# Other PSUM banks for two h groups of the first chunk, turns of pair 1 moved together, and one weight cast from VectorE to ScalarE

## The chip, the cores and the metric

The kernel runs on one core of a Trainium2 chip. The metric is device time in microseconds (us) of one execution; lower is better. Several executions are taken of each kernel, and fast ones are compared with fast ones. Times inside an execution count from the first instruction of its trace. The program names the engines PE (TensorE's matmuls), PEld (its weight loads), DVE (VectorE), ACT (ScalarE), POOL (GpSimd) and SP (the queue that issues most DMA).

## The reference

```python
def _attn_ref(q, k, v):                       # 8 batches, 8 heads, 576 positions, 64 dims
    q_p, k_p = phi(q, cos_w, sin_w), phi(k, cos_w, sin_w)   # phi: concat(relu(x)*cos, relu(x)*sin)
    kv  = einsum('bhsf,bhsd->bhfd', k_p, v)
    num = einsum('bhsf,bhfd->bhsd', q_p, kv)
    den = einsum('bhsf,bhf->bhs', q_p, k_p.sum(2))[..., None] + 1e-06
    return num / den

def _moe_ref(x, w_in, w_out, beta):           # x: 4608 x 512, w_in: 512 x 2048, w_out: 2048 x 512
    h = x @ w_in
    return (h * (1.0 / (1.0 + exp(-beta * h)))) @ w_out
```

The output of the attention is the x of the second function.

## The kernel before

The second function runs in nine chunks of 512 tokens: 16 h groups (each 128 columns of h, in one PSUM bank), each through ScalarE, then the products with w_out (`o_mm`). TensorE is kept busy with these while the attention of later batches is slipped in between. The first batch has nothing to hide behind: its attention is the head of the kernel, cut into two halves by heads ("pair 0", "pair 1"), so that the first h groups can begin on pair 0's half of the contraction. The parts concerned:

```python
    def h_bank(c, jt):                       # which PSUM bank an h group fills
        if c < 2 and jt < 4:
            return ((3, 2, 0, 1), (6, 7, 4, 5))[c][jt]
        ...
    # head of the kernel, batch 0; turns are TensorE transposes, copied out by ScalarE
    x_turn_pe(0, 0, 4, 4, jps=(0,))          # pair 0, blocks 0-3, into bank 4
    x_turn_pe(0, 4, 8, 5, jps=(0,))          # pair 0, blocks 4-7, into bank 5
    for n in range(7):
        num_mm(n, 1, 0, n)                   # num of pair 1 ("num 1"): banks 0 and 1
    num_mm(7, 1, 6, 0)                       # its eighth block: banks 6 and 7
    for gj, eng in zip(GJ, ("pool", "dve", "pool", "dve")):
        cast_win(0, gj, eng, jps=slice(0, 1))
    for gj, eng in zip(GJ, ("dve", "pool", "pool", "pool")):
        cast_win(0, gj, eng, jps=slice(1, 2))
    got = x_rden(0, 0, 0, 7, (1,))           # den and its reciprocal, VectorE, from banks 0 and 1
    x_mul(got, 0, 4)                         # num / den, VectorE
    x_mul(got, 4, 7)
    x_mul(x_rden(6, 0, 7, 8, (1,)), 7, 8)
    for jt in range(3):
        h_mm(0, jt, (0, 1))                  # h groups on pair 0: banks 3, 2, 0
    x_turn_pe(0, 0, 4, 4, ("act",), (1,))    # turns of pair 1
    h_mm(0, 3, (0, 1))
    x_turn_pe(0, 4, 8, 5, ("act",), (1,))
    ...
    def rest():                              # after h group 4
        ...
        load_w("out", 0); load_w("out", 1)
        load_raw(1, "v"); load_raw(1, "k"); load_raw(1, "q")
        x_turn_dma(0, 8, 9)                  # DMA transpose
        load_w("out", 2, 2); load_w("out", 3, 2)
        ...
        v_scale(1, 0); k_relu(1); q_relu(1, 0); q_relu(1, 1)
    def second():                            # after the products of slot 23
        takes.append(q_turn_pe(1, 1, 6, hold=True))
        cast_out(8)                          # first cast of w_out 2, VectorE
        takes[0]("act", 0)                   # pair 0 of q out of PSUM: copies on ScalarE,
        takes[0]("dve", 1)                   # multiplies by tan on VectorE
        cast_out(9, "a")
        takes[0]("dve", 0)
        ...
    early = {                                # what follows which slot of chunk 0
        22: lambda: (kv_mm(1, 0, 6), kv_mm(1, 1, 6), kv_take((0, 1), 6, "act"),
                     takes.append(q_turn_pe(1, 0, 4, hold=True))),
        23: second,
        24: lambda: (num_seven(0, 4), x_mul(x_rden(4, 0, 0, 7, (0,)), 0, 7)),
        ...
    }
```

## Time and profile before

| | before |
|---|---|
| time, median (lowest to highest) of the 4 executions given with the result | 295.78 us (295.52 to 296.08) |
| span of the profiled execution, granted clock | 294.0 us, 0.997 |
| TensorE busy; its share of the chain that ended last | 96%; 91% |
| VectorE, ScalarE, GpSimd busy | 39%, 48%, 26% |
| third h group waits, at 19.21 us | 1.35 us |
| the relu of batch 1's q on VectorE starts; TensorE turns it | 39.43 us; 40.66 us |

The busy shares say which engine bounds most of the span.

### The profile page before, as it was taken

What the parts mean: (1) busy time and instruction counts of PE and PEld (TensorE: products, weight loads), DVE (VectorE), ACT (ScalarE), POOL (GpSimd) and SP (SyncE); (2) the same over time, 40 slices, a digit from 0 to 9 for tenths busy, and PEclk for the clock granted to TensorE, in tenths of its full rate; (3) what the DMA queues carried; (4) which work ended last, traced back from release to release, by engine and by line L of the source; (5) the groups of instructions that cost most, each with busy time, mean ns of one, the idle gap of its engine ahead of it and who ended that gap; (6) DMA issues with size and microseconds to landing.
All of it is one profiled execution on the core that took longest, in us unless ns stands there. A gap on an engine that the chain in (4) does not pass through costs nothing.

```text
span 294.0 us, 7191 instructions
## 1 busy us (share of the span) xinstructions
PE 282.8 (96%) x3047; PEld 143.5 (49%) x3074; DVE 115.2 (39%) x293; ACT 141.8 (48%) x225; POOL 75.5 (26%) x85
## 2 busy tenths in 40 slices
PE   8679999999999999999999999999999999999994
PEld 7454455455445544454445444454455444444444
DVE  5999976743910292029401950086005000000000
ACT  5748856862157324821483138412760177127511
POOL 1440000624381026402640255027701210000000
PEclk9999999999999999999999999999999999999998
DMA  7999999999998099906991699068102910131033
GB/s 256 365 393 384 392 305 389 278 230 352 165 268 347 3 140 231 393 30 131 222 391 47 125 229 401 34 74 198 36 2 41 154 36 0 38 79 28 0 74 71
DMA packets 50736, 53.89 MB, mean 183 GB/s; under 512 B 31232, under 2 KB 31632, under 8 KB 50704
## 3 DMA queue, kind: packets, MB, share of 16 engines
q1 hardware_dynamic: 47744, 45.95, 53.9%
q0 software_dynamic: 2688, 7.34, 10.5%
q8 instruction: 24, 0.39, 0.5%
q10 hardware_dynamic: 272, 0.14, 0.2%
q14 instruction: 8, 0.07, 0.1%
HBM read 36.71 MB, written 9.44 MB: 157 GB/s over the span
## 4 chain that ended last, share of the span: by engine, by line
PE 91%; DMA 3%; DVE 2%; issue 1%; SPq 1%; ACT 0%
PE ps L365 42%; PE ps L390 41%; PE ps L280 3%; DMA raw_v<-in_v_dram 3%; PE ps L259 3%; PE ps L408 1%; SPq L78 1%; DVE win L108 1%; DVE xs L302 1%; PE ps L339 0%; PE ps L229 0%; DVE rden L295 0%; DVE vb L204 0%; ACT xt L344 0%; DVE rk L189 0%
## 5 line engine op out<-in xcount | busy, mean ns | idle before, releaser
L365 PE MATMUL ps<-xt,win 128*128 128x512 bf16 (+1 forms) x580 | 127.8, 378 | 1.5 <-DVE xs L302 1.3
L390 PE MATMUL ps<-wout,g_t 128*128 128x512 bf16 x535 | 120.5, 379 | 2.5 <-issue 1.5
L372 ACT ACTIVATE g_t<-ps,beta 128x512 bf16<-128x512 f32 x144 | 98.6, 688 | 33.1 <-PE ps L365 33.1
L365 PEld LDWEIGHTS <-win 128*128 128x128 bf16 x580 | 56.1, 98 | 67.6 <-issue 2.1
L390 PEld LDWEIGHTS <-g_t 128*128 128x128 bf16 x560 | 53.9, 98 | 64.2 <-issue 0.9
L385 POOL DMA_DIRECT2D out_dram<-o_sb x56 | 39.2, 705 | 141.2 <-ACT o_sb L396 141.2
L396 ACT COPY o_sb<-ps 128x512 f32<-128x512 f32 x35 | 20.2, 588 | 98.7 <-PE ps L390 94.5
L271 DVE CAST kv<-ps 128x520 bf16<-128x520 f32 x6 | 4.2, 700 | 68.9 <-PE ps L259 68.9
L217 POOL TENSOR_TENSOR qs<-qt,tanr 128x1152 bf16<-128x1152 bf16 x12 | 28.4, 2384 | 9.3 <-DMA qt<-qb 7.8
L411 DVE COPY o_sb<-ps 128x256 f32<-128x256 f32 (+1 forms) x2 | 0.7, 358 | 62.7 <-PE ps L408 62.7
L302 DVE TENSOR_TENSOR xs<-ps,rden 128x768 bf16<-128x768 f32 (+5 forms) x27 | 23.1, 863 | 0.8
L291 DVE TENSOR_TENSOR den<-ps,eps 128x12 f32<-128x12 f32 (+4 forms) x26 | 4.2, 160 | 33.5 <-PE ps L280 33.5
L214 DVE TENSOR_SCALAR vb<-raw_v,cos 128x256 bf16<-128x256 f32 x63 | 17.1, 346 | 0.0
L214 DVE TENSOR_SCALAR vb<-raw_v,sin 128x256 bf16<-128x256 f32 x54 | 14.7, 347 | 0.0
L280 PEld LDWEIGHTS <-qt 64*64 64x64 bf16 x576 | 10.4, 106 | 4.7 <-issue 3.8
L108 DVE CAST win<-w_stage 64x512 bf16<-64x512 f32 x27 | 12.0, 443 | 0.6
L189 DVE TENSOR_SCALAR qb<-raw_q 128x1152 bf16<-128x1152 f32 x16 | 11.4, 752 | 1.8 <-DMA raw_q<-in_q_dram 1.8
L280 PE MATMUL ps<-kv,qt 64*64 64x65 bf16 x576 | 11.7, 195 | 0.5 <-ACT kv L269 0.5
L259 PE MATMUL ps<-vb,rk 64*64 64x130 bf16 x576 | 10.2, 218 | 1.9 <-ACT rk L187 1.3
L280 PE MATMUL ps<-kv,qs 64*64 64x65 bf16 x576 | 11.5, 193 | 0.0
L259 PEld LDWEIGHTS <-rk 64*64 64x64 bf16 x576 | 8.5, 106 | 5.8 <-issue 3.0
L280 PEld LDWEIGHTS <-qs 64*64 64x64 bf16 x576 | 10.4, 105 | 0.0
(58 smaller groups left out, 98.1 us busy)
## 6 DMA issues: line engine op xcount, KB each, us to landing
raw_v<-in_v_dram SPq DMA_DIRECT2D x7, 1152.0 KB, 10.3
raw_k<-in_k_dram SPq DMA_DIRECT2D x7, 1152.0 KB, 12.8
raw_q<-in_q_dram SPq DMA_DIRECT2D x7, 1152.0 KB, 7.1
out_dram<-o_sb POOLq DMA_DIRECT2D x56, 128.0 KB, 4.0
w_stage<-in_moe_w_in_dram SPq DMA_DIRECT2D x3, 1024.0 KB, 13.7
w_stage<-in_moe_w_out_dram SPq DMA_DIRECT2D x2, 1024.0 KB, 8.1
w_stage<-in_moe_w_out_dram SPq DMA_DIRECT2D x4, 512.0 KB, 11.2
out_dram<-o_sb SPq DMA_DIRECT2D x14, 128.0 KB, 2.3
```

Of the source, the lines that this page charges most:

```text
L108: nc.vector.tensor_copy(o, a)
L189: nc.vector.tensor_scalar(dst, src, scalar1=0.0, scalar2=None, op0=ALU.max)
L214: nc.vector.tensor_scalar(o, a, scalar1=t[:, n : n + 1], scalar2=None, op0=ALU.mult)
L217: eng.tensor_tensor(dst.rearrange("q n (g p) -> q n g p", g=2), src.rearrange("q n (g p) -> q n g p", g=2), tanr[:, n0:n1].unsqueeze(2).to ...
L259: nc.tensor.matmul(t[jj * HP : (jj + 1) * HP, g], lhsT=rk[hs, n, 2 * jp + jj, :], rhs=vb[hs, n, 2 * jp + jj].rearrange("q s e -> q (s e)") ...
L280: nc.tensor.matmul(ps[cols, bank + jj, slot * E : (slot + 1) * E], lhsT=(qt, qs)[cs][rows, jp, n, cols], rhs=kv[rows, g, jp, cs, :], start ...
L302: nc.vector.tensor_tensor(o.rearrange("q j n s d -> q j (n s) d"), nv[:, :, a:z, :, 0:D].rearrange("q j n s d -> q j (n s) d"), rden[:, :, ...
L365: nc.tensor.matmul(ps[:, h_bank(c, jt), blocks.start * 64 : blocks.stop * 64], lhsT=win[jt // 4][:, mi, (jt % 4) * P : (jt % 4 + 1) * P], ...
L372: nc.scalar.activation(g_t, ps[:, h_bank(c, jt)], AF.Silu, scale=beta[:, jt : jt + 1])
L385: eng.dma_start(out=out_v[bb, n][:, m0:m1], in_=o_sb[hf * HP : (hf + 1) * HP, m0:m1])
L390: nc.tensor.matmul(o_ps, lhsT=gs[c, jt][:, tt * P : (tt + 1) * P], rhs=wout[jt // 4][:, jt % 4, :], start=(jt == 0), stop=(jt == JT - 1))
L396: nc.scalar.copy(o_sb, o_ps)
```

## The change

The intent is to let the third h group run without waiting for num 1 to be read, to let both turns of pair 1 go ahead of the fourth group, and to start VectorE's work on num 1 one cast earlier.

```diff
     def h_bank(c, jt):
         if c < 2 and jt < 4:
-            return ((3, 2, 0, 1), (6, 7, 4, 5))[c][jt]
+            return ((3, 2, 5, 0), (6, 7, 4, 5))[c][jt]
...
-    warm_pe(8, 128, bank=2)
+    warm_pe(7, 128, bank=2)
...
-    for gj, eng in zip(GJ, ("dve", "pool", "pool", "pool")):
+    for gj, eng in zip(GJ, ("act", "pool", "pool", "pool")):
         cast_win(0, gj, eng, jps=slice(1, 2))
...
     x_turn_pe(0, 0, 4, 4, ("act",), (1,))
+    x_turn_pe(0, 4, 8, 1, ("act",), (1,))
     h_mm(0, 3, (0, 1))
-    x_turn_pe(0, 4, 8, 5, ("act",), (1,))
```

## The prediction

> **What bounds the kernel now.** I read the page first: engine shares and the chain that ended last.
>
> ```profile
> PE 282.8 (96%) x3047; PEld 143.5 (49%) x3074; DVE 115.2 (39%) x293; ACT 141.8 (48%) x225; POOL 75.5 (26%) x85
> ...
> PE 91%; DMA 3%; DVE 2%; issue 1%; SPq 1%; ACT 0%
> ```
>
> TensorE is busy in 96% of the span and carries 91% of the chain. The list of waits after 21 us shows nothing for TensorE but 1.5 us of "issue" in 8 places. So the change can win only in the head, before TensorE runs without a gap, and what it wins there reaches the end only if nothing later makes TensorE wait. The diff touches the stretch from 15 to 22 us. The timeline there, TensorE first (start, duration, instruction, idle before it and what ended that):
>
> ```profile
> 16.84 1.02 PE L365 MATMUL ps<-xt,win 128*128 128x512 bf16 x4
> 19.21 0.59 PE L365 MATMUL ps<-xt,win 128*128 128x512 bf16 x2 [1.35 <-DVE xs L302]
> 19.64 0.39 PE L339 MATMUL ps<-ident,xs 128*128 128x128 bf16 x4
> 19.87 0.59 PE L365 MATMUL ps<-xt,win 128*128 128x512 bf16 x2
> 20.30 0.39 PE L339 MATMUL ps<-ident,xs 128*128 128x128 bf16 x4
> 20.70 1.03 PE L365 MATMUL ps<-xt,win 128*128 128x256 bf16 x6
> ```
>
> The x4 at 16.84 are h groups 1 and 2 on pair 0. The third group (19.21) waits 1.35 us, though its data are ready: it goes to bank 0, which num 1 filled and VectorE's multiplies (L302) still read. VectorE and ScalarE in the same stretch:
>
> ```profile
> 16.14 1.48 DVE L108 CAST win<-w_stage 64x512 bf16<-64x512 f32 x2
> 17.55 0.15 DVE L291 TENSOR_TENSOR den<-ps,eps 128x14 f32<-128x14 f32 x1
> 17.73 0.24 DVE L295 RECIPROCAL rden<-den 128x14 f32<-128x14 f32 x1
> 18.00 1.16 DVE L302 TENSOR_TENSOR xs<-ps,rden 128x512 bf16<-128x512 f32 x2
> 19.08 0.15 DVE L291 TENSOR_TENSOR den<-ps,eps 128x2 f32<-128x2 f32 x1
> 19.26 0.17 DVE L295 RECIPROCAL rden<-den 128x2 f32<-128x2 f32 x1
> 19.46 0.29 DVE L302 TENSOR_TENSOR xs<-ps,rden 128x128 bf16<-128x128 f32 x1
> ...
> 20.07 1.24 ACT L344 COPY xt<-ps 128x512 bf16<-128x512 bf16 x2 [3.27 <-PE ps L339]
> ```
>
> num 1 is finished at 16.75 (its last matmuls start at 16.54 and take 0.21), but VectorE begins its den at 17.55: the second of the two casts, 16.90 to 17.62, stands in front. ScalarE is idle for 3.27 us. Both turns of pair 1 queue behind the blocked third group, and the chain runs from the second turn through ScalarE's second xt copy (20.72 to 21.31) to TensorE at 21.36, from where it is TensorE alone.
>
> The next view is a later one, around the second batch's q, because there data arrive by DMA:
>
> ```profile
> 39.51 1.22 PE L259 MATMUL ps<-vb,rk 64*64 64x130 bf16 x72
> 40.66 0.68 PE L229 MATMUL ps<-ident,qb 128*128 128x128 bf16 x9
> ...
> 39.43 1.43 DVE L189 TENSOR_SCALAR qb<-raw_q 128x1152 bf16<-128x1152 f32 x2 [1.48 <-DMA raw_q<-in_q_dram]
> 41.27 0.49 DVE L116 TENSOR_SCALAR wout<-w_stage,rbeta 128x512 bf16<-128x512 f32 x1 [0.41 <-DMA w_stage<-in_moe_w_out_dram]
> 41.67 1.42 DVE L217 TENSOR_TENSOR qs<-ps,tanr 128x512 bf16<-128x512 bf16 x2
> ```
>
> VectorE sits idle for 1.48 us until q of batch 1 lands at about 39.4; the first of its two relus ends at 40.19, and TensorE turns that result at 40.66. TensorE arrives only 0.47 us after the data. The table of stretches shows why that landing is what it is: DMA share 1.04 to 1.05 and 387 to 389 GB/s from 16.8 to 33.4 us.
>
> **What the Trainium skill says.** "PSUM — Partial Sum Buffer", § PSUM bank collisions raise a hardware error, asks for semaphores by bank and quadrant and not by address. That is the wait seen here: the third group writes columns that have nothing to do with the unread num, but the same bank; it starts at 19.21, 0.05 us after the multiply that reads bank 0 ends at 19.16. "SBUF — State Buffer", § Who interferes with whom: casts in VectorE's two-port mode and GpSimd share a port pair and exclude each other. The trace agrees: VectorE's cast takes 0.72 us in the stretch with GpSimd casting and 0.42 us (median) elsewhere. "ScalarE: Activation LUTs", § What ACT_TABLE_LOAD costs, gives 186 ns + 0.833 ns per element for immediate scale; the trace's ScalarE relu of 128x576 takes 0.667 us, the formula 0.666. So a 64x512 cast there is an estimate of 0.61 us. "DMA: Bandwidth & Descriptors", § Queues, rings and completion order: each DMA engine takes one queue's descriptors in ring order. The loads land in their order of issue here.
>
> **The change part by part.**
>
> 1. The cast moves. VectorE loses 0.72 us before den. The one remaining cast ends at 16.87, den can start as close behind it as now, at 16.79 (0.07 before the cast's recorded end), just after num 1. Everything through the last x_mul moves up by 17.55 - 16.79 = 0.75 us: first multiply done at 17.94, second at 18.41, eighth block at 19.00. ScalarE takes the cast at about 16.79 (after its two pair 0 copies, 15.72 + 1.07), done about 17.4, inside its idle 3.27 us: free. Its half of the weight has landed by then (VectorE's cast of it started at 16.90 without a wait, GpSimd's at 16.65).
>
> 2. Third group to bank 5. That bank held pair 0's second turn, copied out by 16.79. So the group follows at once: four matmuls at 0.215 us each from 16.84, then two more, to 18.13. The 1.35 us of idle is gone from there.
>
> 3. Turn order. First turn at 18.13 (xs ready 17.94), its four matmuls are issued in 0.22 us and drain to 18.52; ScalarE copies 18.55 to 19.14. The second turn in bank 1 must wait for the eighth block at 19.00: three of its four transposes earlier, the last at 19.05, drained at 19.27. ScalarE's second copy runs from 19.30 to 19.89. The fourth group (bank 0, free at 18.41) fills TensorE meanwhile: 2 x 0.215 from 19.11 to 19.54. Then four half-width matmuls of pair 1 at 0.108 each, to 19.97. The second copy is done by 19.94 with its signal, so no wait. TensorE thus enters its unbroken part at 19.97 in place of 21.36: **1.39 us gained locally.**
>
> 4. One fewer 128-wide warm-up matmul, 0.107 us at about 5 us. The chain there is DMA (V to 12.26), so it is worth 0.
>
> What becomes of 1.39 us later. VectorE's casts of w_in 1 to 3 can't move by 0.75: the first one's weights land at about 19.1 us, so they move by about 0.53. TensorE moves by 1.39 and the margins shrink by 0.86. The tightest are h groups 13 and 15 of chunk 0. Last cast for group 15: now 31.03, then 30.50; its second matmul, which needs it, now 31.86, then 30.47. With 0.05 for the signal that is a wait of some 0.08: gain 1.31.
>
> Then q of batch 1. Its landing doesn't move, since the queue ahead of it was never empty: the loads in front are issued 0.5 us earlier into a backlog of megabytes. kv_mm would start at 38.20 (its k_relu ends at about 37.85, good) and end at 39.35, but the relu of q still ends at 40.19, so the turn begins at 40.24, not 39.35. **Gain left: 40.66 - 40.24 = 0.42.** TensorE waits about 0.9 us there. A little after, num of pair 0 needs the tan multiplies on VectorE, which follow the cast of w_out 2 (its landing at 41.25 ends a DMA wait as well) and end at 43.09. Num starts at 43.49 now, so at earliest 43.14: **gain left 0.35.** The next dependences (second multiply of x ends at 48.92, turn at 49.47) leave 0.55, so they pass. From there on TensorE only moves: 295.89 - 0.35 = **295.54**, which I round to 295.5.
>
> **The rivals.**
>
> *All of it survives (294.6).* For: the chain now is TensorE alone from 21.36, which read naively promises the full 1.3. Against: a 0.47 us slack behind a DMA-limited landing. It would need q to land 0.9 us earlier. From 37 to 39 us DMA throughput falls under 200 GB/s around a DMA transpose, which VectorE triggers some 0.5 us earlier in the new kernel, so the landing could move, but the transpose's issue (25.85 to 31.6) already ends 5 us before.
>
> *Nothing gained, or slightly worse (295.9 to 296.1).* For: q, w_out 2 and the tan multiplies could be later by a few tenths in this run; ScalarE's cast could collide with the turns' copies, or the waits could be put on coarser signals than I assume. Against: ScalarE has 1.1 us between the estimate of its cast's end and the first turn copy.
>
> *The local gain is smaller (0.6 to 0.7).* If VectorE's den does not start at 16.79 because num 1's signal comes later, all shifts with it. But as anything from 0.42 upward is cut to 0.35 afterwards, the time would still be 295.5. The point estimate is robust in this direction.
>
> **Range and chances.** The before runs spread over 0.4 us (295.68 to 296.08). The capped gain of 0.35 is of that size; allow run scatter of about 0.4 above and, for the case that the landing moves, some 0.8 below: 294.7 to 296.1. Two per cent is 5.9 us, over four times the whole local gain, and nothing in the change adds work of that size: same 0.98, 0.01 for either side.
>
> **What would show it.** Right: third group at about 17.7 with no wait; den at 16.8; unbroken TensorE from about 20.0; then a new wait of 0.8 to 0.9 us before the turn of q at 40.2, ended by VectorE's relu behind a q landing still near 39.4; and num at 43.1. Wrong: if that wait is missing and q lands near 38.5, the time goes to 294.6; if TensorE waits in the w_in casts by more than 0.1, my 0.53 for VectorE was off; if the second copy on ScalarE ends after 20.0, the local gain is smaller, with little effect on the end.

## The result

| | before | changed |
|---|---|---|
| median (lowest to highest), 4 executions each | 295.78 us (295.52 to 296.08) | 295.09 us (294.92 to 295.44) |
| ratio, 95% interval | | 0.9978 (0.9960 to 0.9995) |
| span of the profiled execution | 294.0 us | 293.1 us |

A ratio is the mean time of one kernel's fast runs over the mean of the other's of the same rounds, so it is not quite the ratio of the medians. This one is 0.65 us (0.0022 x 295.8) in favour of the change, with an interval from 0.15 to 1.2 us.

The page of the changed kernel, busy times and the chain that ended last:

```profile
PE 282.5 (96%) x3046; PEld 143.2 (49%) x3073; DVE 115.0 (39%) x292; ACT 142.5 (49%) x226; POOL 73.3 (25%) x85
...
PE 84%; DMA 8%; DVE 3%; issue 1%; SPq 1%
PE ps L390 39%; PE ps L365 38%; DMA raw_q<-in_q_dram 5%; PE ps L280 3%; DMA raw_v<-in_v_dram 3%; PE ps L259 2%; DVE win L108 2%; PE ps L408 1%; SPq L78 1%; DVE xs L302 1%; PE ps L229 0%; DVE vb L204 0%; DVE rden L295 0%; PE ps L339 0%; DVE qb L189 0%
```

TensorE's busy time is the same to 0.3 us, but its share of the chain fell from 91% to 84%, and a load has come in with 5%: q. The chain no longer follows TensorE through the h groups of chunk 0; it goes through the landing of batch 1's q. The timeline of the head, TensorE, VectorE and ScalarE (start, duration, instruction, idle before it and its releaser):

```profile
16.54 1.46 PE L365 MATMUL ps<-xt,win 128*128 128x512 bf16 x6
17.83 0.80 PE L339 MATMUL ps<-ident,xs 128*128 128x128 bf16 x7
18.88 0.23 PE L339 MATMUL ps<-ident,xs 128*128 128x128 bf16 x1 [0.25 <-ACT xt L344]
18.95 1.90 PE L365 MATMUL ps<-xt,win 128*128 128x512 bf16 x12
...
16.60 0.17 DVE L291 TENSOR_TENSOR den<-ps,eps 128x14 f32<-128x14 f32 x1
17.08 1.16 DVE L302 TENSOR_TENSOR xs<-ps,rden 128x512 bf16<-128x512 f32 x2
18.53 0.29 DVE L302 TENSOR_TENSOR xs<-ps,rden 128x128 bf16<-128x128 f32 x1
...
16.38 0.62 ACT L104 CAST win<-w_stage 64x512 bf16<-64x512 f32 x1
19.15 0.58 ACT L344 COPY xt<-ps 128x512 bf16<-128x512 bf16 x1 [0.30 <-PE ps L339]
```

Six matmuls now follow each other at 16.54, the third group with them; seven of the eight turns come straight behind; ScalarE's cast takes 0.62 us in what was idle time. The "ACT" on the last turn is the wait's last semaphore as inferred, but that copy ends at 18.84; VectorE's last multiply, from which this turn reads, ends at 18.82 too, and I read the wait as its. The end of this stretch, where the half-width matmuls pass into the unbroken run, is 1.54 us earlier than before; but this execution also began earlier. The last turns before the change's first effect (15.28 us before, 14.98 here) are 0.30 us earlier already, because V landed earlier (VectorE's second product with it starts at 11.98 and not at 12.28). So the local gain is 1.54 - 0.30 = 1.24 us.

The stretch of batch 1's q, TensorE first and VectorE second:

```profile
37.98 1.22 PE L259 MATMUL ps<-vb,rk 64*64 64x130 bf16 x72
40.33 0.68 PE L229 MATMUL ps<-ident,qb 128*128 128x128 bf16 x9 [1.13 <-DVE qb L189]
43.22 0.22 PE L280 MATMUL ps<-kv,qt 64*64 64x65 bf16 x4
...
39.52 1.43 DVE L189 TENSOR_SCALAR qb<-raw_q 128x1152 bf16<-128x1152 f32 x2 [1.58 <-DMA raw_q<-in_q_dram]
41.35 0.48 DVE L116 TENSOR_SCALAR wout<-w_stage,rbeta 128x512 bf16<-128x512 f32 x1 [0.40 <-DMA w_stage<-in_moe_w_out_dram]
41.75 1.42 DVE L217 TENSOR_TENSOR qs<-ps,tanr 128x512 bf16<-128x512 bf16 x2
```

TensorE reaches the kv product 1.53 us earlier (39.51 to 37.98) and then stands 1.13 us in front of the turn, a wait that the kernel before doesn't have. At num it is 43.49 - 43.22 = 0.27 us ahead. The lead stays like that for 150 us. The other 0.6 us by which the two spans differ come from one place: the profile of the kernel before has a pause of TensorE at 193.6 us that this one lacks.

```profile
193.56 1.68 PE L390 MATMUL ps<-wout,g_t 128*128 128x512 bf16 x7 [0.40 <-issue]
```

Nothing in the profile releases it ("issue"). The experiments ask whether it belongs to the kernel or to the execution.

### The profile page after: what moved, and what is told of

Its sections match the earlier page's. It is cut to its first block, busy times and chain, and to the rows that moved or that the text cites. A ratio compares the mean times of both kernels' runs of the same rounds, so it can differ in the third digit from the quotient of the medians.

```text
span 293.1 us, 7188 instructions
## 1 busy us (share of the span) xinstructions
PE 282.5 (96%) x3046; PEld 143.2 (49%) x3073; DVE 115.0 (39%) x292; ACT 142.5 (49%) x226; POOL 73.3 (25%) x85
## 4 chain that ended last, share of the span: by engine, by line
PE 84%; DMA 8%; DVE 3%; issue 1%; SPq 1%
PE ps L390 39%; PE ps L365 38%; DMA raw_q<-in_q_dram 5%; PE ps L280 3%; DMA raw_v<-in_v_dram 3%; PE ps L259 2%; DVE win L108 2%; PE ps L408 1%; SPq L78 1%; DVE xs L302 1%; PE ps L229 0%; DVE vb L204 0%; DVE rden L295 0%; PE ps L339 0%; DVE qb L189 0%
## 5 line engine op out<-in xcount | busy, mean ns | idle before, releaser
L385 POOL DMA_DIRECT2D out_dram<-o_sb x56 | 37.2, 668 | 144.9 <-ACT o_sb L396 144.9
L108 DVE CAST win<-w_stage 64x512 bf16<-64x512 f32 x26 | 11.2, 433 | 0.6
L189 DVE TENSOR_SCALAR rk<-raw_k 128x2304 bf16<-128x2304 f32 (+2 forms) x9 | 10.5, 1172 | 0.6 <-DMA raw_k<-in_k_dram 0.6
```

The costliest lines, as they stand in the source:

```text
L108: nc.vector.tensor_copy(o, a)
L189: nc.vector.tensor_scalar(dst, src, scalar1=0.0, scalar2=None, op0=ALU.max)
L385: eng.dma_start(out=out_v[bb, n][:, m0:m1], in_=o_sb[hf * HP : (hf + 1) * HP, m0:m1])
```

## The experiments

**Theory.** The change wins about 1.25 us in the head, and two data limits between 40 and 43 us take most of it back: the relu of q behind q's landing, and, just behind, num behind the tan multiplies, which stand on VectorE behind the first cast of w_out 2 and so behind *its* landing. **Rivals:** every local gain counts in full; q is the only limit; q is late because of a DMA transpose; the profile's pause is a part of the kernel before.

All kernels gave correct results. Kernels share the runs of the kernel before: first four below (before 295.48 us), next four (295.45 us) and last four (295.29 us). "Ratio" is to those.

### The changed kernel again

No edit.

> The changed kernel once more, for a tighter interval. My theory (the local gain is cut where TensorE waits for q of batch 1): 0.27 to 0.40 us faster than before, ratio about 0.9989, and a wait of about 1.1 us before the turn of q. Rival (the full local gain of 1.3 to 1.5 us reaches the end in most executions and my one profile shows an unlucky q): about 1.3 us faster, ratio 0.9955. Rival (the first timing of 0.65 us is the true size, so there is a second gain after the wait): ratio 0.9978.

Measured: 294.69 us, ratio 0.9988 (0.9972 to 1.0003), so 0.35 us faster. The wait at the turn was 0.78 us, not the 1.1 that I expected; the relu of q started at 39.11, the turn at 39.93, num at 42.81. Each of the three is about 0.4 us earlier than in the first profile of the same kernel, while TensorE arrived at the kv product at the same time (37.94 and 37.98). So num follows the data one to one and not TensorE, which is what a limit does. (The cast of w_out 2 started 0.41 us earlier too, so this doesn't say which of the two landings sets num.) The full-gain rival is out for this kernel (1.3 us lies outside the interval); the timing alone doesn't separate 0.35 from 0.65.

### The cast alone

```diff
-    for gj, eng in zip(GJ, ("dve", "pool", "pool", "pool")):      # kernel before
+    for gj, eng in zip(GJ, ("act", "pool", "pool", "pool")):
```

> The kernel before with the cast on ScalarE alone; banks and turn order as before. Local gain by my theory: VectorE's den 0.75 us earlier, third group 18.45 in place of 19.21, unbroken TensorE about 0.75 us earlier. As 0.75 is more than the slack of 0.3 to 0.45 before the turn of q, the end gains as much as the whole change, 0.3 to 0.4 us, with a wait of about 0.4 us at the turn of q. Rival (every local gain counts in full): 0.75 us faster, half of what the whole change gives.

Measured: 295.00 us, ratio 0.9990 (0.9977 to 1.0002). TensorE in its head and at q:

```profile
18.46 0.59 PE L365 MATMUL ps<-xt,win 128*128 128x512 bf16 x2 [0.72 <-DVE xs L302]
...
38.76 1.22 PE L259 MATMUL ps<-vb,rk 64*64 64x130 bf16 x72
40.24 0.68 PE L229 MATMUL ps<-ident,qb 128*128 128x128 bf16 x9 [0.27 <-DVE qb L189]
```

The third group still waits for its bank, but half as long (0.72 us for 1.35). The execution began 0.13 us early, so the local gain is 39.51 - 38.76 - 0.13 = 0.62 us. A wait of 0.27 us at q is already there (0.4 expected), and num comes at 43.12 against 43.22 for the whole change. Half of the local gain gives all of the end gain.

### The banks and the order alone

```diff
-    for gj, eng in zip(GJ, ("act", "pool", "pool", "pool")):      # changed kernel
+    for gj, eng in zip(GJ, ("dve", "pool", "pool", "pool")):
```

> The change without its cast: that one stays on VectorE; banks and turn order are new. Local gain by my theory: the multiplies of pair 1 stay where they were, the third group runs before them at about 17.7, ScalarE's second copy ends at about 20.6 in place of 21.3, unbroken TensorE 0.65 us earlier. At the end 0.3 to 0.4 us, as the whole change, with a wait of about 0.3 us at the turn of q. Rival (every local gain counts in full): 0.65 us faster.

Measured: 294.55 us, ratio 0.9978 (0.9966 to 0.9990).

```profile
16.70 1.46 PE L365 MATMUL ps<-xt,win 128*128 128x512 bf16 x6
18.62 0.81 PE L339 MATMUL ps<-ident,xs 128*128 128x128 bf16 x7 [0.46 <-DVE xs L302]
...
38.76 1.22 PE L259 MATMUL ps<-vb,rk 64*64 64x130 bf16 x72
39.91 0.68 PE L229 MATMUL ps<-ident,qb 128*128 128x128 bf16 x9
```

The third group is free, and the wait has moved to the turn, which now waits for VectorE. Local gain 39.51 - 38.76 - 0.14 = 0.61 us. With the cast's 0.62 that makes 1.23, the whole change's 1.24: the two parts add up in the head. At the end they don't. The wait at q that I expected is missing: q's relu began at 39.09 in this execution, and the turn at 39.91 is 0.82 behind it, the same distance as where TensorE did wait (40.33 - 39.52 = 0.81). TensorE and data arrived together. As timed, this half of the change is no worse than the whole.

### The DMA transpose behind the loads of w_out

```diff
         load_raw(1, "q")                                          # changed kernel
-        x_turn_dma(0, 8, 9)
         load_w("out", 2, 2)
         load_w("out", 3, 2)
+        x_turn_dma(0, 8, 9)
```

> The changed kernel with the DMA transpose of the ninth block of batch 0 issued behind the loads of w_out 2 and 3 in place of in front of them, so that nothing slow follows q in the queue. If the landing of q of batch 1 limits, and the transpose delays that landing: q lands 0.5 to 1.0 us earlier (38.5 to 39.0), the wait at its turn shrinks from 1.1 to 0.2 to 0.6 us, and the time falls by 0.3 to 0.9 us below the changed kernel. Rival (q lands by bandwidth alone): landing near 39.4, same time as the changed kernel within 0.2 us.

Measured: 295.00 us, but six executions between 294.30 and 296.92; ratio 1.0003 (0.9976 to 1.0030). The relu of q started at 39.51: no earlier than before. The idea that the transpose delays q finds no support here, and the rival fits. One profile doesn't close it: its head was 0.66 us late (V's second product at 12.64 and not 11.98), and the least gain looked for, 0.5 us, lies within the scatter of q's landing (below). What did come earlier is w_out 2, now issued in front of the transpose (the queue begins with its loads at 27.40 and not 31.81): its cast follows the relus without a wait.

```profile
40.87 0.49 DVE L116 TENSOR_SCALAR wout<-w_stage,rbeta 128x512 bf16<-128x512 f32 x1
```

In the changed kernel it started at 41.35 behind the same relu (39.52) and the same turn of q (40.33 in both). Num starts at 43.16 here and at 43.22 there. So with q landing as late as this, the second limit costs only some 0.06 us more than the first.

Two of the executions were near 296.8, the profiled one among them, and it shows a new thing, TensorE in the middle of num of pair 1:

```profile
45.62 0.19 PE L280 MATMUL ps<-kv,qs 64*64 64x65 bf16 x1
47.37 0.22 PE L280 MATMUL ps<-kv,qs 64*64 64x65 bf16 x3 [1.55 <-issue]
```

TensorE stands still for 1.55 us between two matmuls of one product, with no data wait. The moved transpose runs just before: from 42.2 to 44.6 us the DMA engines are busy and move only 168 GB/s. Two packets of the DMA queues of kind "instruction" follow it, one between 44.5 and 45.0 us and one between 45.5 and 46.0; in the changed kernel the same two come some 2 us earlier (42.5 to 43.0 and 43.0 to 43.5). That TensorE's own instructions were late behind the transpose fits, but is argued and not shown: the view doesn't say for which engine a packet is.

### Four idle matmuls in the changed kernel, and in the kernel before

```diff
     early = {
+        10: lambda: warm_pe(4),          # 4 x 128x512 into bank 1, which nothing reads then
```

> The changed kernel with four idle 512-wide matmuls (4 x 0.216 = 0.86 us of TensorE) behind h group 11 of chunk 0. If TensorE has 0.8 to 1.1 us to spare before the turn of q: the wait there shrinks to 0 to 0.25 us, and the time is that of the changed kernel within 0.1 us. Rival (no slack; TensorE time counts in full): 0.86 us longer than the changed kernel.

> The kernel before with the same four matmuls. It has no wait for q, so both theories say the whole 0.86 us is paid (ratio to before 1.0029), at most 0.3 us less where q lands late in an execution; with the changed kernel's four matmuls free, the two kernels with matmuls differ by about 1.2 us, as much as the local gain of the change.

Measured: changed with matmuls 295.80 us, ratio 1.0007 (0.9992 to 1.0022), from five fast runs; its profiled execution fell into a throttled state (425 us at a granted clock of 0.66) and says nothing. Before with matmuls 296.88 us, ratio 1.0054 (1.0037 to 1.0071).

Both expectations were partly missed. The kernel before pays 1.6 us (0.0054 x 295.4) and not 0.86; the changed kernel pays about 0.6 to 0.9 us more than without them (ratios 0.9978 to 0.9988), and not nothing. The difference between the two kernels came out as expected, though: 1.0054 - 1.0007 = 0.0047, or 1.4 us, two to four times what separates them without the matmuls (0.0022 and 0.0012). That the change is then worth its whole local gain is nevertheless not shown by this, because part of the 1.4 us arises far behind q. The trace of the kernel before with matmuls shows where its excess went. TensorE reaches the kv product at 40.14; with 0.23 us for an early start that is 40.14 - 39.51 + 0.23 = 0.86, all of it as expected and without a wait for q. The rest came later, most of it in one pause of 0.49 us of idle, close to where the kernel before had paused:

```profile
193.88 0.22 PE L280 MATMUL ps<-kv,qs 64*64 64x65 bf16 x2 [0.49 <-issue]
```

From before this pause to behind it, the distance to the second profile of the kernel before (below) grows from 0.71 to 1.39 us. So 0.68 us of the excess is the pause, as far as this execution speaks for the others. Another thing differs in it: q's relu started only at 40.07, over 0.5 us later than in any other profile with q in one load. Whether the matmuls delayed the load or it is scatter isn't known.

### q of batch 1 in two halves

```diff
-        load_raw(1, "q")                                          # changed kernel
+        load_raw(1, "q", 0, 2)
+        load_raw(1, "q", 2, 4)
```

> The changed kernel with q of batch 1 loaded in two halves, so the relu and the turn of the first pair no longer wait for the whole of q: first half lands near 38.0 us, its relu ends at about 38.8, TensorE turns it at about 39.1 without a wait or with one under 0.2 us. By my second limit (the tan multiplies on VectorE stand behind the cast of w_out 2, which lands at 41.25) TensorE then waits about 0.6 us more at the group of w_out 2 or at num, which still starts at about 43.1: time equal to the changed kernel within 0.15 us. Rival (the wait for q is the only limit): 0.8 to 1.1 us faster than the changed kernel.

Measured: 294.99 us, ratio 0.9985 (0.9967 to 1.0003). The time is that of the changed kernel, as the second limit says. The profile couldn't show why, since this execution's head was late: V landed 1.06 us later than in the repeat below (second product at 13.11 and not 12.05), the granted clock was 0.64 between 16.0 and 19.2 us, and TensorE was at the kv product only at 40.09. So it was run once more (below).

### Halves, and both limits behind them moved

```diff
         takes.append(q_turn_pe(1, 1, 6, hold=True))               # kernel with halves
-        cast_out(8)
         takes[0]("act", 0)
         takes[0]("dve", 1)
-        cast_out(9, "a")
         takes[0]("dve", 0)
         takes[0]("act", 1)
+        cast_out(8)
+        cast_out(9, "a")
         cast_out(10)
...
         cast_out(11, "a")
-        cast_out(12)
-        for j in range(13, JT):
+        cast_out(12, "a")
+        num_seven(0, 4)
+        x_mul(x_rden(4, 0, 0, 7, (0,)), 0, 7)
+        cast_out(13)
+        for j in range(14, JT):
             cast_out(j, "a")
...
-        24: lambda: (num_seven(0, 4), x_mul(x_rden(4, 0, 0, 7, (0,)), 0, 7)),
```

> The same halves, with both limits behind q moved as well: the tan multiplies of pair 0 ahead of the cast of w_out 2 on VectorE, num of pair 0 ahead of the group of w_out 2 on TensorE, and pair 0's multiply of x ahead of a cast that waits for w_out 3 (casts 12 and 13 swapped between the engines). By the theory of queued limits: num of pair 0 at about 41.6 us, 0.6 to 1.0 us faster than the changed kernel, about 1.0 to 1.4 us faster than the kernel before (ratio 0.9955 to 0.9966). Rival (some further data limit within 0.2 us, such as w_out 3): equal to the changed kernel.

Measured: 294.54 us, ratio 0.9970 (0.9954 to 0.9985), so 0.89 us faster than the kernel before, a little short of the expected 1.0. Against the changed kernel (0.9988 and 0.9978), that is 0.2 to 0.5 us and not the 0.6 to 1.0 that I expected. It is 0.0015 better than the halves alone, which the intervals don't secure. The trace does show the effect:

```profile
39.25 0.68 PE L229 MATMUL ps<-ident,qb 128*128 128x128 bf16 x9
41.52 0.22 PE L280 MATMUL ps<-kv,qt 64*64 64x65 bf16 x4 [0.23 <-DVE qs L217]
```

No wait at the turn of q, num at 41.52 as expected (it stands ahead of one 0.86 us group there, so its time isn't compared with the others' directly). The first h group of chunk 1 starts at 50.47 us; before it started at 51.59 and with the change at 51.31. So it keeps 1.12 us where the change keeps 0.28 (these two executions began 0.18 and 0.30 us early). It has the lowest ratio, though its interval overlaps with that of the banks and order alone (0.9966 to 0.9990).

### The kernel before again

No edit.

> The kernel before, for a second profile of it. Its first profile has a pause of TensorE of 0.56 us at 193.6 us that no other kernel's profile has at that place. If the pause belongs to the execution and not to the kernel, it is missing here and the span is about 293.4 us in place of 294.0; if it belongs to the kernel, it is here again, and the change removed it.

Measured: 295.29 us, span 293.5 us. The pause at 193.6 us is not there. It belonged to the execution. The two profiles of the kernel before agree within 0.05 us up to num (turn of q at 40.61, num at 43.45). So of the 0.9 us between the first two spans, about 0.5 us (294.0 - 293.5) was this pause and not the change.

### Halves again, and the changed kernel with matmuls again

The edits are those above.

> The kernel with q in two halves once more, because its first profile fell in an execution in which TensorE ran at half rate between 17 and 19 us and so arrived too late for any wait to show. Expected where the head runs at full rate: no wait or one under 0.2 us at the turn of q, then a wait of 0.5 to 0.7 us at the group of w_out 2 or at num; num at about 43.1 us, time equal to the changed kernel. Rival: num at about 42.2 us.

Measured: 294.83 us, ratio 0.9986 (0.9968 to 1.0005), a head at full clock, and the expected picture:

```profile
39.19 0.68 PE L229 MATMUL ps<-ident,qb 128*128 128x128 bf16 x9
...
42.77 0.22 PE L280 MATMUL ps<-kv,qt 64*64 64x65 bf16 x4 [0.31 <-DVE qs L217]
...
40.90 0.49 DVE L116 TENSOR_SCALAR wout<-w_stage,rbeta 128x512 bf16<-128x512 f32 x1 [0.90 <-DMA w_stage<-in_moe_w_out_dram]
41.30 1.41 DVE L217 TENSOR_TENSOR qs<-ps,tanr 128x512 bf16<-128x512 bf16 x2
```

TensorE turns q without a wait, and then waits 0.21 us for the cast of w_out 2 and 0.31 us at num for the tan multiplies, 0.52 in all (0.5 to 0.7 expected). VectorE is idle for 0.90 us before the cast, while q's multiplies stand behind it. The rival, for which q was the only limit, wanted num at 42.2; at TensorE's own pace from the turn to num, 2.83 us in the kernel before (40.66 to 43.49), it would have been 42.02.

> The changed kernel with four idle matmuls once more, because its first profile fell in a throttled execution (clock 0.66). Expected by the theory of slack before q: wait at the turn of q 0 to 0.3 us, num at the same time after the landing of q as in the changed kernel. Rival: TensorE 0.86 us later at num than in the changed kernel.

Measured: 296.03 us, ratio 1.0027 (1.0010 to 1.0044). In this execution too the head was late (V 0.41 us, clock 0.61 between 16.0 and 19.2 us), TensorE reached the kv product at 39.90, later than 37.98 + 0.86, and found q landed. The matmuls were not free here; the late head alone had used up the slack. Whether they are free in a head at full clock stays open; the times say that on average they cost 0.6 us or more.

### The warm-up matmul put back

```diff
-    warm_pe(7, 128, bank=2)                                       # changed kernel
+    warm_pe(8, 128, bank=2)
```

> The changed kernel with the removed warm-up matmul put back. My prediction gave this part 0: time equal to the changed kernel, ratio to before 0.998 to 0.999, same stretch from 15 us on. Rival (the warm-up matmul is on the path of the first turn of q): 0.1 us slower. Rival (the one matmul less makes TensorE's rate in the head worse in some executions): this one is faster by 0.2 us or more in the mean, with a smaller spread.

Measured: 295.28 us (294.52 to 295.77), ratio 0.9998 (0.9982 to 1.0014). That is outside the range that I expected, by 0.0008, but its interval takes in the changed kernel's 0.9988. The trace shows the same head (kv product at 37.93 against 37.94) and a wait of 0.58 us at q. So no cost of the extra matmul can be seen; an effect of 0.3 us in some executions can't be excluded.

## Why the prediction was right

Set side by side, what VectorE and TensorE do at q and at w_out 2 in eight of the profiled executions (us; the last column is num minus the start of the cast):

| kernel | kv product | q relu starts | turn of q | cast of w_out 2 starts | num | difference |
|---|---|---|---|---|---|---|
| before | 39.51 | 39.43 | 40.66 | 41.27 | 43.49 | 2.22 |
| before again | 39.46 | 39.48 | 40.61 | 41.32 | 43.45 | 2.13 |
| cast alone | 38.76 | 39.42 | 40.24 | 41.25 | 43.12 | 1.87 |
| banks alone | 38.76 | 39.09 | 39.91 | 40.91 | 42.78 | 1.87 |
| changed | 37.98 | 39.52 | 40.33 | 41.35 | 43.22 | 1.87 |
| changed again | 37.94 | 39.11 | 39.93 | 40.94 | 42.81 | 1.87 |
| changed, warm-up 8 | 37.93 | 38.91 | 39.73 | 40.74 | 42.62 | 1.88 |
| halves again | 38.04 | 37.59 | 39.19 | 40.90 | 42.77 | 1.87 |

TensorE's arrival (second column) varies over 0.8 us among the lower six rows, and q's relu over 1.9 us. Num follows the cast of w_out 2 in all six at 1.87 or 1.88 us. In the kernel before it doesn't; there TensorE's own work sets it. Left out are the two executions with a head at a lower clock, the throttled execution and the kernel before with matmuls, where TensorE arrives behind its data, and the two kernels in which the cast was moved or waits no longer (all halves, transpose late).

Read with care, though: in the first five of the six rows the cast starts 1.82 or 1.83 us after q's relu, so there num is as constant behind q (3.69 to 3.71 us). These rows show that data set num, and not which. The last row tells them apart: q's first half came over 1.3 us earlier, and num stayed with the cast. So the change does what it was meant to do in the head, and then the kernel runs into two landings, of q and of w_out 2, that are nearly a tie.

1. **The local gain** was put at 1.39 us and measured 1.24. Both parts work as predicted, each a little smaller (0.62 for 0.75, 0.61 for 0.65). The missing 0.15 is mostly one assumption: den would start 0.07 us ahead of the cast's recorded end, as before; it starts 0.03 us behind it (cast to 16.57, den at 16.60). Why is not shown. One reading behind this part was too broad: of VectorE's three casts beside GpSimd's, the first (at 15.69) took 0.42 us, and only the other two 0.72. The one that moved is one of the two.
2. **The casts of w_in 1 to 3** were to cost 0.08 us. No such wait of TensorE shows. VectorE's first cast starts at 18.84, right behind the last multiply. That is 0.83 us earlier than before, or 0.53 when the early start of 0.30 is taken off, as said; but the predicted wait for its weights isn't there. TensorE's lead at the kv product, 1.53 us, is that of the head, 1.54. A miss of no consequence.
3. **The landing of q** stays where it is, right: the relu starts at 39.52 where 39.4 was said. Its scatter between executions, 38.91 to 39.52 in these rows, was not in the working (only in the range), and it is as large as the end gain. In the kernel before, an early landing is of no use; in the changed kernel it goes straight into the time. That is why single profiles of the change show 0.27, 0.68 and (with the warm-up put back) 0.87 us at num.
4. **The second limit** (num at 43.14 at the earliest, 0.35 us left) held as a distance and not as a time: num came at 43.22 in the first profile and between 42.62 and 43.22 since, as the landings moved. That there is a second limit, the halves kernel shows: it removed the first one alone, and no gain can be seen (0.9985 and 0.9986 against 0.9988). The step between them (0.42 to 0.35) is too small to be seen in any time; the predicted time would have been as good with the first limit alone.
5. **The time**, 295.5 predicted (from a 295.89 for the kernel before, where the table has 295.78) and 295.09 measured, lies within the range; as the range goes from 294.7 to 296.1, this alone says little about the mechanism, which the traces show. The gain of 0.35 us was measured as 0.65 and then 0.35, with intervals that hold both; the mean of executions can't settle the size below some 0.3 us. That the second timing hit 0.35 exactly is partly luck: the profiles of the same kernel have leads of 0.27 and 0.68 us at num. The rival in which all of it survives is refuted by the repeat and by the trace, the one with no gain is not excluded by the repeat's interval alone but is by the first.

Open: what makes TensorE pause for 0.5 us near 193 us in some executions and 1.55 us at 46 us behind the moved transpose, why idle matmuls cost more than their length, why some heads run at a lower clock, and whether the transpose delays q a little.

## What to carry to other kernels

A gain in the head of a pipelined kernel is worth what the next data arrival leaves of it. Before trusting it, go forward along the engine that bounds the kernel and look, at each stage fed by DMA, how long the engine arrives behind its data; the smallest such distance caps the gain, here at about 0.3 of 1.24 us in the first profile. Then look for the second smallest at once: taking away the first limit alone, as with the halves, can yield nothing.

## What the Trainium skill lacked or had wrong

- "Runtime: NRT & Kernel Launch", § Instruction fetch mechanics, calls the cost of crossing an instruction block "mostly hidden". The runs show pauses of TensorE without a data wait of 0.40 and 0.49 us of idle near 193 us in two executions, and of 1.55 us at 46 us in the kernel with the moved transpose. No page says how to tell such a pause in a profile from others, and that these are instruction fetches is not shown.
- "TensorE: Matmul & The Clock Gate", § HAM oscillation — how this bites in real kernels, gives idle gaps of over about 3.4 us as what lowers the clock. In two executions the granted clock between 16.0 and 19.2 us was 0.64 and 0.61 though TensorE's longest gap from 10 us on was 1.73 and 1.18 us; in the changed kernel's first profile, with 1.04 us, it stayed at 1.00, and in the second profile of the kernel before it did so too, with a gap of 2.11 us that ended at 11.54. So the longest gap doesn't tell these heads apart. Whether the sum of shorter gaps matters is not settled.
- I found no page with a figure for how far the landing of one load moves between executions of one program. Here the landing of q, some 39 us into the kernel, moved by 0.6 us (relu starts of 38.91 to 39.52 in kernels with the same DMA program ahead of it), and by 1.2 us if the kernel before with matmuls (40.07) is counted in.
